# The products of P with V, formed in 16 wide matmuls per batch with four slabs of P as one stationary operand

## The chip, the core and the metric

The kernel runs on one NeuronCore of a Trainium2 chip. The metric is the time of one execution on the device, in microseconds (us); 121.49 us is the median of three runs before the change (121.39 to 121.63). TensorE (PE in the profile) multiplies a stationary operand, which it loads first (PEld), with a moving operand and adds up in PSUM. VectorE is DVE, ScalarE is ACT, GpSimd is POOL, and SyncE (SP) issues nearly all of the loads.

## The reference

One decoding step: 8 sequences (batch b), one query position each, 32 query heads in 8 key/value heads of 4, head size 128, and a window of the last 1024 of 4096 cached positions.

```python
xn = _layernorm(x)                                   # x: [8, 1, 512]
q  = (xn @ wq) as [8, 32 heads, 1, 128]
k, v = the last W = 1024 positions of k_cache, v_cache, each head repeated 4 times
p  = softmax(q @ k.T * 128 ** -0.5)
s  = (p @ v) as [8, 1, 4096] @ wo
g  = silu((gelu(xn @ w_gate) * (xn @ w_up)) @ w_down)
out = x + s * g
```

All inputs are bf16. The caches in the window are 2 MB of K and 2 MB of V for each batch.

## The kernel before

The order of instructions on every engine is the order in which the program is written (a manual schedule), and each engine works in that order. Buffers come from pools that turn round; the framework puts in the semaphore waits.

**Loads.** Every large load goes through SP's queue: K and V of a batch in two pieces of 1 MB each (line 73; g = 0 and 1, four key/value heads each), the weights in pieces of 1 to 2 MB. They land in a ring of eight slots of 2 MB, `slot(name)`. A slot is loaded again when its last reader is done: for a K slot that is the second `turn_k` of its batch on DVE, for a V slot the products of its batch on PE. Besides that, the loads share eight completion semaphores, and a load is issued only when the load that used its semaphore before has landed.

**Layout.** A slot holds a batch so that partition p has C = 32 positions (c) of one key/value head of each of two head groups g; it is head p % 4 of the group. One slab is the 128 values of one c. The scores of a batch lie in one PSUM tile, 1024 columns of 128 partitions, in which partition 32 j + h has query head h at a quarter j of the positions, for all four key/value heads of a group; columns of heads that are not its own are set to minus 1e30 (L285). DVE's transposes of 32 x 32 blocks make `kT` of K and `pT` of the exponentials `P_sb`.

**The loop over batches.** With b the batch whose softmax is formed, the body of the loop issues

```python
        load_k(b + 2); load_v(b + 1); turn_k(b + 1, 0)   # SP; SP; DVE L235
        softmax(b)            # DVE L306, L311, L313; ACT L316 four times, L318
        scores(b + 1, 0)      # PE L285 twice, L296 eight times
        gather(b - 1)         # PE L361, L365
        turn_k(b + 1, 1); scores(b + 1, 1)               # DVE L235; PE L296
        turn_p(b)             # DVE L329
        values(b)             # PE L340
        keep_o(b)             # ACT L353
```

and after batch 4 also `regroup(0)` (DVE L376, L378, PE L389, DVE L392), which divides the outputs of batches 0 to 3 by the sums and turns them for the product with `wo`.

**Products with V.** `values(b)` goes over two groups and 32 slabs. For slab c the stationary operand is a 128 x 32 piece of `pT` (32 query heads; the weight is zero where a partition holds a key/value head that is not the query head's own) and the moving operand is the slab's 128 columns of V. The output goes to the 32 partitions that start at 32 (c % 4), so four matmuls that follow each other use four separate quarters of the array's columns; eight slabs are added up in each quarter. `O_ps` has two buffers of one PSUM bank. `keep_o` copies its 128 x 256 values to `O_sb` (fp32), and `gather` adds the four quarters and picks the group's own heads by multiplying with a selection matrix `sel` in fp32; line 365 does the same for the sums of the softmax.

**After the loop** come `gather(7)`, `regroup(1)`, then the feed-forward part: `z_ps` and `u_ps` (L451), the GELU chain on ACT and DVE (L461 to L474), `f_ps` (L480), the sigmoid part (L488 to L492), the product with `wo` in four parts of 32 matmuls (L499), y and out (L507, L509) and the store (L511). PE does `z_ps` only after `r_ps` of `regroup(1)`.

Of the kernel before, what the change touches and what calls it, by code (L numbers as in the profile page):

```python
# [8 lines left out]
ALU = mybir.AluOpType  # L9
AX = mybir.AxisListType  # L10
BF16 = mybir.dt.bfloat16
FP32 = mybir.dt.float32
I32 = mybir.dt.int32
PSUM = bass.MemoryType.PSUM
# [7 lines left out]
def kernel(  # L22
# [13 lines left out]
    nc = tc.nc  # L36

    B, Sq, D = A_x.shape
    Hkv, Sk, Dh = A_k_cache.shape[1], A_k_cache.shape[2], A_k_cache.shape[3]
    Hq = A_wq.shape[1] // Dh  # L40
# [5 lines left out]
    P = nc.NUM_PARTITIONS  # L46
    NK = D // P
    HG = 4
    NG = Hkv // HG
    C = W * HG // P  # L50
# [6 lines left out]
    consts = ctx.enter_context(tc.tile_pool(name="consts", bufs=1))  # L57
    keep = ctx.enter_context(tc.tile_pool(name="keep", bufs=1))
    two = ctx.enter_context(tc.tile_pool(name="two", bufs=2))
    ring = ctx.enter_context(tc.tile_pool(name="ring", bufs=N_SLOTS))  # L60

    def slot(name):
        return ring.tile([P, 2 * ROW], BF16, name=name, tag="slot")
# [17 lines left out]
    k_sb, v_sb = {}, {}  # L81
# [10 lines left out]
    for i in range(2):  # L92
        t = slot("wq_sb").rearrange("p (k n) -> p k n", k=NK // 2)
# [6 lines left out]
    ident = consts.tile([P, P], BF16, name="ident")  # L100
    nc.vector.memset(ident, 0.0)
    nc.gpsimd.affine_select(
        out=ident,
        in_=ident,
# [13 lines left out]
        out=xpad,  # L118
        in_=xpad,
# [17 lines left out]
        out=xhat,  # L137
# [9 lines left out]
    with tc.tile_pool(name="ps_x", bufs=1, space=PSUM) as ps_x:  # L147
# [7 lines left out]
        for t in range(4):  # L155
# [4 lines left out]
                start=True,  # L160
                stop=True,
# [5 lines left out]
    qd = Hq // NG  # L167
# [6 lines left out]
        out=hv,  # L174
        in_=hv,
# [7 lines left out]
        out=neg_st,  # L183
        in_=neg_st,
# [8 lines left out]
        out=neg_mv,  # L193
        in_=neg_mv,
# [7 lines left out]


    NU = Hq // 8
    sel = consts.tile([P, NG, Hq], FP32, name="sel")
    nc.vector.memset(sel, 0.0)
    for g in range(NG):
        nc.vector.tensor_reduce(
            out=sel[:, g, g * qd : (g + 1) * qd],
            in_=ident.rearrange("p (t g h) -> p g h t", t=4, g=NG)[:, g],  # L210
            axis=AX.X,
            op=ALU.add,
        )
    own = consts.tile([P, 8], FP32, name="own")
    nc.vector.tensor_reduce(
        out=own, in_=ident.rearrange("p (i e) -> p e i", e=8), axis=AX.X, op=ALU.add
    )
    pick = consts.tile([P, 4 * NU], BF16, name="pick")
    with nc.allow_low_precision(reason="sums of zeros and a single one"):
        nc.vector.tensor_reduce(  # L220
            out=pick, in_=ident.rearrange("p (a e) -> p a e", e=8), axis=AX.X, op=ALU.add
# [22 lines left out]
    with tc.tile_pool(name="ps_q", bufs=1, space=PSUM) as ps_q:  # L244
        q_ps = [ps_q.tile([P, 512], FP32, name=f"q_ps{i}") for i in range(8)]
        for k in range(NK):
            for i in range(8):
# [4 lines left out]
                    start=(k == 0),  # L252
                    stop=(k == NK - 1),
# [19 lines left out]
    pT, S, P_sb, O_ps = {}, {}, {}, {}  # L273
    sums = keep.tile([P, B], FP32, name="sums")

    actx = ExitStack()
    ps_s = actx.enter_context(tc.tile_pool(name="ps_s", bufs=2, space=PSUM))
    ps_o = actx.enter_context(tc.tile_pool(name="ps_o", bufs=2, space=PSUM))
    ps_g = actx.enter_context(tc.tile_pool(name="ps_g", bufs=1, space=PSUM))

    def scores(b, g):
# [50 lines left out]
        )  # L332

    def values(b):
        O_ps[b] = ps_o.tile([P, NG, Dh], FP32, name="O_ps")
        for g in range(NG):
            vv = v_sb[b][:, g].rearrange("p (c d) -> p c d", d=Dh)
            for c in range(C):
                t = c % 4
                nc.tensor.matmul(  # L340
                    O_ps[b][32 * t : 32 * t + 32, g, :],
                    pT[b][:, c // 2, :, c % 2],
                    vv[:, c, :],
                    start=(c < 4),
                    stop=(c >= C - 4),
                )

    o_ps = {}
    O_sb = {}

    def keep_o(b):
        O_sb[b] = two.tile([P, NG, Dh], FP32, name="O_sb")
        nc.scalar.copy(out=O_sb[b], in_=O_ps[b])  # L353

    def gather(b):
        q = b % 4
        if q == 0:
            o_ps[b // 4] = ps_g.tile([P, Dh + 1], FP32, name="o_ps")
        o = o_ps[b // 4][32 * q : 32 * q + 32, :]
        for g in range(NG):  # L360
            nc.tensor.matmul(  # L361
                o[:, 0:Dh], sel[:, g, :], O_sb[b][:, g, :], start=(g == 0), stop=(g == NG - 1)
            )
        for g in range(NG):
            nc.tensor.matmul(  # L365
                o[:, Dh : Dh + 1],
                sel[:, g, :],
                sums[:, b : b + 1],
                start=(g == 0),
                stop=(g == NG - 1),  # L370
            )

    def regroup(q):

# [24 lines left out]
    for b in range(B):  # L399
        if b + 2 < B:  # L400
            load_k(b + 2)
        if b + 1 < B:
            load_v(b + 1)
            turn_k(b + 1, 0)
        softmax(b)
        if b + 1 < B:
            scores(b + 1, 0)
        if b >= 1:
            gather(b - 1)
        if b + 1 < B:  # L410
            turn_k(b + 1, 1)
            scores(b + 1, 1)
        turn_p(b)
        values(b)
        keep_o(b)
        if b == 4:
            regroup(0)
# [10 lines left out]
    for u in range(NU):  # L428
        if u % 2 == 0:
            pair = slot("wo_sb").rearrange("p (v j d) -> p v j d", v=2, d=D)  # L430
        t = pair[:, u % 2]
# [6 lines left out]
        wo.append(t)  # L438

    gather(B - 1)  # L440
    regroup(1)
    actx.close()
# [4 lines left out]
    for n, ws in (("z_ps", wgu[0]), ("u_ps", wgu[1])):  # L447
        ps = ps_f.tile([P, FT], FP32, name=n)
        for k in range(NK):
            for t in range(4):  # L450
# [4 lines left out]
                    start=(k == 0),  # L455
                    stop=(k == NK - 1),
# [6 lines left out]
        out=z2, in0=z2, scalar1=0.044715, scalar2=1.0, op0=ALU.mult, op1=ALU.add  # L463
# [11 lines left out]
        out=hT.rearrange("p j b -> p (j b)"), in_=h_bf.rearrange("p (y j) -> p j y", j=NJ)  # L475
    )
    f_ps = ps_f.tile([P, DT], FP32, name="f_ps")
    for j in range(NJ):
        for t in range(4):
# [4 lines left out]
                start=(j == 0),  # L484
                stop=(j == NJ - 1),
# [4 lines left out]
        out=g_sb, in0=g_sb, scalar1=0.5, scalar2=0.5, op0=ALU.mult, op1=ALU.add  # L490
# [5 lines left out]
    for u in range(NU):  # L496
        for j in range(8):
            for t in range(4):
# [4 lines left out]
                    start=(u == 0 and j == 0),  # L503
                    stop=(u == NU - 1 and j == 7),
# [7 lines left out]
        out=out_f.rearrange("b (t d) -> t b d", t=4), in_=out_sb[0 : P : RB, :]  # L512
# [31 lines left out]
```

## Time and profile before

| | before |
|---|---|
| median of three runs | 121.49 us |
| the profiled execution's own time | 121.48 us |
| its span, first to last instruction | 119.4 us |
| mean granted TensorE clock | 0.838 |
| bytes read from HBM | 47.46 MB, 397 GB/s over the span |
| busy: PE, PEld | 73.0 us (61%), 38.7 us (32%) |
| busy: DVE, ACT, POOL | 75.8 us (63%), 31.4 us (26%), 3.2 us (3%) |

The profiled execution's time is its span and 2.1 us around it. Where lines of the profile are shown, an entry is start and duration in us, then engine, line of the kernel, operation, output and inputs. "x8" counts instructions, a bracket gives the idle time of the engine before the entry and what ended it.

### The profile page before, as it was taken

What the parts mean: (1) busy time and instruction counts of PE and PEld (TensorE: products, weight loads), DVE (VectorE), ACT (ScalarE), POOL (GpSimd) and SP (SyncE); (2) the same over time, 40 slices, a digit from 0 to 9 for tenths busy, and PEclk for the clock granted to TensorE, in tenths of its full rate; (3) what the DMA queues carried; (4) which work ended last, traced back from release to release, by engine and by line L of the source; (5) the groups of instructions that cost most, each with busy time, mean ns of one, the idle gap of its engine ahead of it and who ended that gap; (6) DMA issues with size and microseconds to landing.
All of it is one profiled execution on the core that took longest, in us unless ns stands there. A gap on an engine that the chain in (4) does not pass through costs nothing.

```text
span 119.4 us, 2300 instructions
## 1 busy us (share of the span) xinstructions
PE 73.0 (61%) x985; PEld 38.7 (32%) x992; DVE 75.8 (63%) x101; ACT 31.4 (26%) x75; POOL 3.2 (3%) x10
## 2 busy tenths in 40 slices
PE   0001499811994987969687674991994547545370
PEld 0000134300341544535443351450453433143350
DVE  1048978399739999999959959909943241651000
ACT  2233000676007052341712510700616211200000
POOL 2006100000000000000000000000000000000000
PEclk9999999985599999999999998599589855555555
DMA  1999999999999999999999999999999999999930
GB/s 47 411 445 417 434 425 431 417 428 434 428 420 425 431 423 423 428 423 431 417 431 420 431 423 423 428 428 423 420 434 439 437 433 418 427 421 417 412 148 3
DMA packets 6254, 47.61 MB, mean 399 GB/s; under 512 B 732, under 2 KB 868, under 8 KB 1124
## 3 DMA queue, kind: packets, MB, share of 16 engines
q1 hardware_dynamic: 6228, 47.46, 94.3%
q8 instruction: 8, 0.13, 0.4%
q10 hardware_dynamic: 16, 0.01, 0.0%
q14 instruction: 2, 0.02, 0.0%
HBM read 47.46 MB, written 0.01 MB: 397 GB/s over the span
## 4 chain that ended last, share of the span: by engine, by line
DMA 85%; DVE 6%; PE 4%; SPq 2%; issue 1%
DMA k_sb<-in_A_k_cache_dram 48%; DMA wo_sb<-in_A_wo_dram 20%; DMA v_sb<-in_A_v_cache_dram 17%; DVE kT L235 4%; PE S_ps L296 2%; PE s_ps L499 1%; SPq L73 1%; DVE mx L306 1%; SPq L94 1%; PE O_ps L340 1%; PE r_ps L389 1%; DVE y L507 0%; DVE out_sb L509 0%; DVE oT L392 0%; DVE m L311 0%
## 5 line engine op out<-in xcount | busy, mean ns | idle before, releaser
L296 PE MATMUL S_ps<-kT,qbd 128*128 128x512 bf16 x128 | 34.1, 413 | 15.5 <-DVE kT L235 11.9
L235 DVE STREAM_TRANSPOSE kT<-k_sb 128x2048 int32<-128x2048 int32 x16 | 36.5, 2289 | 4.4 <-DMA k_sb<-in_A_k_cache_dram 4.3
L296 PEld LDWEIGHTS <-qbd 128*128 128x128 bf16 x128 | 12.8, 102 | 31.9 <-issue 16.4
L248 PE MATMUL q_ps<-wq_sb,xnR 128*128 128x512 bf16 x32 | 9.8, 481 | 4.3 <-DMA wq_sb<-in_A_wq_dram 4.3
L316 ACT ACTIVATE nb<-m 32x1 f32<-32x1 f32 x32 | 6.4, 201 | 22.5 <-DVE m L313 22.2
L306 DVE TENSOR_REDUCE mx<-S_ps 128x1 f32<-128x1024 f32 x8 | 9.6, 1196 | 4.1 <-PE S_ps L296 4.1
L318 ACT ACTIVATE P_sb<-S_ps,nb 128x1024 bf16<-128x1024 f32 x8 | 11.1, 1390 | 0.3
L340 PE MATMUL O_ps<-v_sb,pT 128*32 128x128 bf16 x512 | 9.1, 226 | 2.6 <-DVE pT L329 2.6
L340 PEld LDWEIGHTS <-pT 128*32 128x32 bf16 x512 | 7.6, 100 | 5.6 <-issue 3.0
L353 ACT COPY O_sb<-O_ps 128x256 f32<-128x256 f32 x8 | 3.0, 372 | 23.3 <-PE O_ps L340 23.3
L329 DVE STREAM_TRANSPOSE pT<-P_sb 128x512 int32<-128x512 int32 x8 | 5.7, 711 | 3.4 <-ACT P_sb L318 3.3
L248 PEld LDWEIGHTS <-xnR 128*128 128x128 bf16 x32 | 3.7, 118 | 10.1 <-issue 8.1
L361 PE MATMUL o_ps<-O_sb,sel 128*32 128x128 f32 x32 | 6.3, 332 | 0.9 <-ACT O_sb L353 0.9
L499 PE MATMUL s_ps<-wo_sb,oT 128*32 128x128 bf16 x128 | 4.4, 307 | 3.7 <-DMA wo_sb<-in_A_wo_dram 3.7
L258 ACT CAST q_both<-q_ps 128x512 bf16<-128x512 f32 x6 | 3.0, 611 | 12.2 <-PE q_ps L248 12.2
L151 PE MATMUL xnT_ps<-ident,xhat 8*128 8x8 bf16 x4 | 0.3, 174 | 8.9 <-DVE xhat L136 8.9
L499 PEld LDWEIGHTS <-oT 128*32 128x32 bf16 x128 | 3.5, 136 | 4.7 <-issue 4.5
L361 PEld LDWEIGHTS o_ps<-O_sb,sel 128*32 128x32 f32 x32 | 3.4, 128 | 5.0 <-issue 1.7
L507 DVE TENSOR_TENSOR y<-s_ps,g_sb 128x128 f32<-128x128 f32 x1 | 0.3, 292 | 7.2 <-PE s_ps L499 7.2
L285 PE MATMUL S_ps<-neg_mv,neg_st 128*128 128x512 bf16 x9 | 3.3, 384 | 1.9 <-DVE q_both L258 1.9
L129 DVE BATCH_NORM_STATS2 stats<-x_sb 8x6 f32<-8x512 bf16 x1 | 0.7, 681 | 5.7 <-DMA x_sb<-in_A_x_dram 5.7
L240 DVE MEMSET qbd<- 128x4096 uint32 x1 | 3.5, 3472 | 0.8 <-issue 0.8
(64 smaller groups left out, 51.2 us busy)
## 6 DMA issues: line engine op xcount, KB each, us to landing
k_sb<-in_A_k_cache_dram SPq DMA_DIRECT2D x16, 1024.0 KB, 19.7
v_sb<-in_A_v_cache_dram SPq DMA_DIRECT2D x16, 1024.0 KB, 20.0
wq_sb<-in_A_wq_dram SPq DMA_DIRECT2D x2, 2048.0 KB, 11.4
wo_sb<-in_A_wo_dram SPq DMA_DIRECT2D x3, 1024.0 KB, 25.1
wgu_sb<-in_B_w_gate_dram SPq DMA_DIRECT2D x1, 1792.0 KB, 21.4
wgu_sb<-in_B_w_up_dram SPq DMA_DIRECT2D x1, 1792.0 KB
wd_sb<-in_B_w_down_dram SPq DMA_DIRECT2D x1, 1792.0 KB
wo_sb<-in_A_wo_dram SPq DMA_DIRECT2D x1, 640.0 KB
```

The costliest lines, as they stand in the source:

```text
L235: nc.vector.transpose(out=t.bitcast(I32), in_=k_sb[b][:, g].bitcast(I32))
L240: nc.vector.memset(qbd, 0.0)
L248: nc.tensor.matmul(q_ps[i], xnR[:, k, :, :].rearrange("p j b -> p (j b)"), wq_sb[k][:, i * 512 : (i + 1) * 512], start=(k == 0), stop=(k = ...
L285: nc.tensor.matmul(S[b][:, half, :], neg_st.rearrange("p j h -> p (j h)"), neg_mv.rearrange("p a n -> p (a n)"), start=True, stop=False,)
L296: nc.tensor.matmul(S[b][:, half, :], qbd[:, m, b, w, g, :], kv[:, half * 16 : (half + 1) * 16, m, :, w], start=False, stop=(g == NG - 1 an ...
L306: nc.vector.tensor_reduce(out=mx, in_=S[b].rearrange("p a c -> p (a c)"), axis=AX.X, op=ALU.max)
L316: nc.scalar.mul(nb[32 * j : 32 * j + 32, :], m1, -inv)
L318: nc.scalar.activation(out=P_sb[b].rearrange("p c i w -> p c w i"), in_=S[b].rearrange("p a (c w i) -> p (a c) w i", w=2, i=32), func=ACT.Exp,
L329: nc.vector.transpose(out=pT[b].rearrange("p c h w -> p (c h w)").bitcast(I32), in_=P_sb[b].rearrange("p c i w -> p (c i w)").bitcast(I32),)
L340: nc.tensor.matmul(O_ps[b][32 * t : 32 * t + 32, g, :], pT[b][:, c // 2, :, c % 2], vv[:, c, :], start=(c < 4), stop=(c >= C - 4),)
L361: nc.tensor.matmul(o[:, 0:Dh], sel[:, g, :], O_sb[b][:, g, :], start=(g == 0), stop=(g == NG - 1))
L499: nc.tensor.matmul(s_ps[32 * t : 32 * t + 32, :], oT[:, j, u, :], wo[u][:, j, t * DT : (t + 1) * DT], start=(u == 0 and j == 0), stop=(u = ...
```

## The change

`values` no longer puts each slab's product into its own quarter. Four slabs of `pT` that follow each other (4 x 32 = 128 columns) are one stationary operand, and the same four slabs of V (4 x 128 = 512 columns) are the moving operand. The output is 128 x 512: four slabs of P against four slabs of V, of which only the four blocks on the diagonal (P of a slab against V of the same slab) are wanted. Eight such matmuls are added up for each group.

`O_ps` becomes two PSUM banks (one for each group) and has one buffer in place of two. `keep_o` takes two copies: the lower 64 partitions with columns 0 to 255 of both groups and the upper 64 with columns 256 to 511, so that each half holds its two diagonal blocks and two unwanted ones. `sel` gains an axis of two, which names the block that is wanted for each row, and is built from wider reductions; a further matrix `sel_s` serves the sums. `gather` then has four matmuls for the outputs, in place of two, and one for the sums, in place of two.

```diff
-    sel = consts.tile([P, NG, Hq], FP32, name="sel")
+    sel = consts.tile([P, NG, 2, Hq], FP32, name="sel")
     nc.vector.memset(sel, 0.0)
     for g in range(NG):
         nc.vector.tensor_reduce(
-            out=sel[:, g, g * qd : (g + 1) * qd],
-            in_=ident.rearrange("p (t g h) -> p g h t", t=4, g=NG)[:, g],
+            out=sel[:, g, :, g * qd : (g + 1) * qd],
+            in_=ident.rearrange("p (a g h w) -> p g w h a", a=2, g=NG, w=2)[:, g],
...
+    sel_s = consts.tile([P, Hq], FP32, name="sel_s")
+    nc.vector.tensor_reduce(
+        out=sel_s, in_=ident.rearrange("p (j h) -> p h j", j=4), axis=AX.X, op=ALU.add
+    )
...
-    ps_o = actx.enter_context(tc.tile_pool(name="ps_o", bufs=2, space=PSUM))
+    ps_o = actx.enter_context(tc.tile_pool(name="ps_o", bufs=1, space=PSUM))
...
     def values(b):
-        O_ps[b] = ps_o.tile([P, NG, Dh], FP32, name="O_ps")
+        O_ps[b] = ps_o.tile([P, NG, 4 * Dh], FP32, name="O_ps")
         for g in range(NG):
-            vv = v_sb[b][:, g].rearrange("p (c d) -> p c d", d=Dh)
-            for c in range(C):
-                t = c % 4
+            vv = v_sb[b][:, g]
+            for c in range(0, C, 4):
                 nc.tensor.matmul(
-                    O_ps[b][32 * t : 32 * t + 32, g, :],
-                    pT[b][:, c // 2, :, c % 2],
-                    vv[:, c, :],
-                    start=(c < 4),
-                    stop=(c >= C - 4),
+                    O_ps[b][:, g, :],
+                    pT[b][:, c // 2 : c // 2 + 2].rearrange("p c h w -> p (c h w)"),
+                    vv[:, c * Dh : (c + 4) * Dh],
+                    start=(c == 0),
+                    stop=(c == C - 4),
                 )
...
     def keep_o(b):
-        O_sb[b] = two.tile([P, NG, Dh], FP32, name="O_sb")
-        nc.scalar.copy(out=O_sb[b], in_=O_ps[b])
+        O_sb[b] = two.tile([P, NG, 2, Dh], FP32, name="O_sb")
+        for a in range(2):
+            rows = slice(64 * a, 64 * a + 64)
+            nc.scalar.copy(
+                out=O_sb[b][rows].rearrange("p g w d -> p g (w d)"),
+                in_=O_ps[b][rows, :, 2 * a * Dh : 2 * (a + 1) * Dh],
+            )
...
         for g in range(NG):
-            nc.tensor.matmul(
-                o[:, 0:Dh], sel[:, g, :], O_sb[b][:, g, :], start=(g == 0), stop=(g == NG - 1)
-            )
-        for g in range(NG):
-            nc.tensor.matmul(
-                o[:, Dh : Dh + 1],
-                sel[:, g, :],
-                sums[:, b : b + 1],
...
+            for w in range(2):
+                nc.tensor.matmul(
+                    o[:, 0:Dh],
+                    sel[:, g, w, :],
+                    O_sb[b][:, g, w, :],
...
+        nc.tensor.matmul(
+            o[:, Dh : Dh + 1], sel_s, sums[:, b : b + 1], start=True, stop=True
+        )
```

More of the change, by code (lines that the diff above doesn't have):

```diff
@@ L360, in gather @@
         for g in range(NG):
-            nc.tensor.matmul(
-                o[:, 0:Dh], sel[:, g, :], O_sb[b][:, g, :], start=(g == 0), stop=(g == NG - 1)
-            )
-        for g in range(NG):
-            nc.tensor.matmul(
-                o[:, Dh : Dh + 1],
-                sel[:, g, :],
-                sums[:, b : b + 1],
-                start=(g == 0),
-                stop=(g == NG - 1),
-            )
+            for w in range(2):
[3 more added lines that the diff above has]
+                    O_sb[b][:, g, w, :],
+                    start=(g == 0 and w == 0),
+                    stop=(g == NG - 1 and w == 1),
+                )
+        nc.tensor.matmul(
+            o[:, Dh : Dh + 1], sel_s, sums[:, b : b + 1], start=True, stop=True
+        )
     def regroup(q):
```

## The prediction

> **What bounds the kernel now.** I read the page's slices and chain first, to see which stage has which limit, then busy time over one batch, then one batch in order of time. On the page:
>
> ```profile
> DVE  1048978399739999999959959909943241651000
> PEclk9999999985599999999999998599589855555555
> DMA  1999999999999999999999999999999999999930
> DMA 85%; DVE 6%; PE 4%; SPq 2%; issue 1%
> ```
>
> The loads never pause from 3 to 115 us and make up 85% of the chain. So 121.5 us is a floor under any change on PE, and the question is how far PE may fall behind the loads before the end moves. One row is a stretch: from the start of a batch's products with V to the next one's (rows 1 to 3), then the last part (columns: length, busy time and count on PE, PEld, DVE, ACT, POOL, granted clock, DMA share, GB/s).
>
> ```profile
> 54.00:60.76 6.76, 5.77 (x91) 3.19 (x91) 5.52 (x6) 2.61 (x7) 0.00 (x0) 1.00 1.01 427
> 68.97:79.22 10.25, 7.83 (x98) 4.15 (x98) 7.26 (x8) 2.62 (x7) 0.00 (x0) 0.83 1.01 424
> 89.07:93.91 4.84, 1.81 (x74) 1.55 (x73) 2.24 (x4) 2.61 (x7) 0.00 (x0) 1.00 1.04 441
> 107.97:119.40 11.43, 4.39 (x128) 3.38 (x127) 1.10 (x4) 0.28 (x1) 0.00 (x0) 0.50 0.59 239
> ```
>
> The loop begins late (first products at 40.48 us), with K already there, and runs at 6.76 us a batch against about 9.9 us in which a batch's 4 MB arrive: it is catching up. From about 61 us it waits for K (kT from 61.08), at 8 to 10 us a batch, to the last products at 93.91. PE has only about 1 us free in a catch-up round. One round in order of time:
>
> ```profile
> 54.00 1.08 PE L340 MATMUL O_ps<-v_sb,pT 128*32 128x128 bf16 x64
> 55.01 0.39 PE L285 MATMUL S_ps<-neg_mv,neg_st 128*128 128x512 bf16 x1
> 55.13 0.37 ACT L353 COPY O_sb<-O_ps 128x256 f32<-128x256 f32 x1 [2.89 <-PE O_ps L340]
> 55.45 1.90 PE L296 MATMUL S_ps<-kT,qbd 128*128 128x512 bf16 x8
> 56.69 0.84 ACT L316 ACTIVATE nb<-m 32x1 f32<-32x1 f32 x4 [1.19 <-DVE m L313]
> 57.28 0.62 PE L361 MATMUL o_ps<-O_sb,sel 128*32 128x128 f32 x4
> 57.56 1.39 ACT L318 ACTIVATE P_sb<-S_ps,nb 128x1024 bf16<-128x1024 f32 x1
> 58.93 1.90 PE L296 MATMUL S_ps<-kT,qbd 128*128 128x512 bf16 x8 [0.93 <-DVE kT L235]
> ```
>
> The 64 small matmuls take 1.0 us in all (54.00 to the next load of weights at 55.00), 16 ns each: four quarters of the array work at once. Eight matmuls with 512 moving columns take 1.83 us to the hand-over (55.45 to 57.28), 0.22 us apart.
>
> **Products with V.** 16 matmuls of 128 x 512 at 0.22 us, the row of the same form, are 3.5 us where 1.0 was: +2.5 us of PE a batch. At the half clock the same row is 0.43 us (16 in 5.35 us at 29.40), so 6.9 us.
>
> [...]
>
> **Gather.** Four instructions of L361 take 0.62 us, 0.115 apart; the new form has four more and two fewer of L365 (0.05 each): +0.36 us, at the half clock (four in 1.06 us, 0.2 apart) +0.6.
>
> **keep_o.** No row is a 64 x 512 fp32 copy. Nearest above: ACT's 128 x 512 cast from PSUM, 0.61 us, six in 3.03, so two make 1.1 us; nearest below: two of the present copy, 0.74. I take 1.1 (+0.75), in the range 0.75 to 1.3. What is queued behind it on ACT is nb and the exponential of the next batch, which now wait for the products on PE. That chain from the start of values(b): 3.5 + 0.17 to the copy, 1.1, nb 0.84, exponential and sum 1.6, transpose of P 0.71, hand-overs 0.2, together 8.1 us to values(b+1).
>
> **The round.** PE: 5.78 + 2.5 + 0.36 = 8.6 us without a gap. DVE needs 6.7 (two transposes of 2.29, 1.19, 0.31, 0.71) and ACT's chain 8.1, so PE takes over as the limit, ACT 0.5 us behind. One O_ps buffer costs nothing: the copy is done 4.8 us into the round, 3.8 us before the next products. K arrives in time.
>
> **Setup.** Two reductions over twice the input, one more, a wider memset: about +0.7 us on DVE before the first kT at 11.68 (rows 0.37 for 128 x 128, 0.25 for 128 x 64). DVE then idles 2.35 us at 22.75, waiting for q. Nothing on the path; +0.7 if that cover were gone.
>
> **Loads.** SP issues a load only when one of its eight semaphores is back; some also wait for values(b). New ends of values(0) to (4): 44.0, 52.6, 61.2, 69.8, 78.4 us, before the issues that need them (46.4, 56.3, 66.0, 76.0, 80.9). Only the third wo load (about 88) waits for values(5), some 3 us more, with up to 16 us of issued loads in front of it. Zero; 3 us if that cover were gone.
>
> **The sum on the profile's times.** Starts of values(0) to (4): 40.5, 49.1, 57.7, 66.3, 74.9 (before: 40.48, 47.24, 54.00, 60.76, 68.97). In the next round regroup(0) sits between: DVE's copy of r_ps waits on PE behind values(4), and kT of batch 6 is queued behind that copy. This row was 10.25 us with part of it at the half clock; with the additions 13.1, or 11.6 if the clock stays up. I take 12.1: values(5) at 87.0, values(6) at 95.6. The last round has no scores and is the ACT chain, 8.1 (4.84 before): values(7) at 103.7 in place of 93.91. Whether those 16 run at full clock is open (3.5 or 6.9):
>
> ```profile
> 70.49:73.90 3.41, 0.99 (x7) 0.49 (x8) 3.22 (x3) 0.00 (x0) 0.00 (x0) 1.00 1.03 430
> 73.90:77.31 3.41, 3.41 (x14) 1.50 (x12) 3.18 (x5) 2.25 (x6) 0.00 (x0) 0.50 0.99 418
> ```
>
> A stretch with PE busy 0.99 of 3.41 us is followed by half clock; the new wait ahead of values(7) holds 1.1 busy us in 4.6, but the stretch may fall otherwise. I take 5.0: end at 108.7 (95.43 before). From there to z_ps was 3.87 us, with copy and gather now 5.1: 113.8 in place of 99.30. z_ps to the end of f_ps is 8.67 us without a wait for loads on the path: 122.4. The four parts with wo, which stood waiting for loads for 3.74 us, now run together: 4 x 1.04 and 0.1, less 0.8 because PE is then busy without a break and may get full clock: 125.9. From there to the end of the span 3.3: 129.2, plus the 2.1 around it: **131.3 us**. The profiled execution, 121.48, is the median's 121.49 within its spread.
>
> **Rivals.** *More than this* (0.12): the copies take 1.3 us and ACT's chain passes PE's (rounds of 8.9), the clock halves at batch 5 and 7. values(5) at 89.6, (7) at 106.8, its end at 113.7, z_ps 119.2: 137 us. For it: the margin of 0.5 us and two half-clock stretches already there. Against it: PE is busier, so that in the loop it idles less.
>
> *The loads cover it, not slower* (0.06): wide matmuls run closer together here than L296 does. The end has 3.74 us of waits for wo to give, of which 1.2 go to copy and gather after values(7). [...] A busier PE with full clock in the last part of L499 (1.25 us) could give 0.6: 120.9. Against it: every run of L296 at full clock has 0.22.
>
> *Not what it says*: 64 small matmuls left in some form. The built order shows 16 pairs a batch of 128 x 512, so I give it none.
>
> **How the numbers follow.** My forecast has 0.82. Its own ends: everything at full clock with copies of 0.75 us gives values(5) at 86.5, values(7) at 102.8 and its end at 106.3, z_ps at 110.9, 0.75 less in the two products behind it (f_ps ends at 118.8), half of 4.2 for wo: 126.3 us. Half clock from batch 5 on gives values(5) at 88.0, values(7) at 104.7, its end at 111.6, z_ps 116.9, f_ps 125.6: 135.3. The range 126.0 to 135.5 takes in both and the near part of the first rival. About 0.2% (0.24 us) is what a measurement here can tell from no change; faster 0.03, same 0.03 (the second rival's halves), slower 0.94.
>
> **What would show it.** Right: rounds of 8.6 us up to values(4) with PE busy throughout; nb waiting for O_sb's copy; DVE idle before kT of batch 6; values(7) starting near 104; no wait for wo before L499, and DMA falling idle at 115 us with the span going on. [...]

## The result and the profile after

The change makes the kernel slower: 129.73 us (median of six runs, 128.58 to 131.14) against 121.49 (six runs, 121.19 to 121.63), a ratio of 1.066 with a 95% interval of 1.061 to 1.071. One of the six runs (131.14) was in a slower state, and the ratio leaves it out; the median of the other five is 129.58 us. The profiled execution took 129.87 us, its span is 127.8. The forecast was 131.3 us, 126.0 to 135.5.

The page, with the same slices and the chain as before:

```profile
DVE  1049975999299939859589445999533020247311
PEclk9999999995999999999999999589999986999559
DMA  2999999999999999999999999999999999991000
PE 66%; DVE 14%; DMA 9%; ACT 4%; issue 2%; SPq 1%; DVEq 0%; ACTq 0%
```

The chain has changed hands: loads were 85% of it, now PE is 66% and loads 9%. The last three slices have no loads and the span goes on. The same stretches as in the prediction, each from one batch's products to the next one's, then from values(7) to z_ps, to the end of f_ps, and to the end of the span (columns as there):

```profile
57.09:65.58 8.49, 8.44 (x45) 4.21 (x45) 6.54 (x7) 3.41 (x8) 0.00 (x0) 1.00 1.02 425
74.06:86.81 12.75, 10.34 (x53) 5.03 (x52) 9.22 (x9) 3.41 (x8) 0.00 (x0) 0.87 1.01 422
95.30:103.24 7.94, 4.65 (x26) 2.46 (x26) 2.24 (x4) 3.39 (x8) 0.00 (x0) 1.00 1.01 426
103.24:113.09 9.85, 7.00 (x34) 3.46 (x35) 1.45 (x2) 1.16 (x2) 0.00 (x0) 0.83 0.99 414
113.09:121.00 7.91, 3.38 (x98) 2.44 (x100) 4.08 (x7) 1.12 (x2) 0.00 (x0) 0.80 0.30 116
121.00:127.80 6.80, 3.42 (x130) 3.15 (x120) 1.10 (x4) 0.28 (x1) 0.00 (x0) 0.73 0.01 4
```

In a catch-up round PE is busy for 8.44 of 8.49 us; DVE has two idle microseconds. One round in order of time, PE and ACT:

```profile
57.09 3.61 PE L343 MATMUL O_ps<-v_sb,pT 128*128 128x512 bf16 x15
...
60.54 0.59 PE L289 MATMUL S_ps<-neg_mv,neg_st 128*128 128x512 bf16 x2
60.74 1.17 ACT L358 COPY O_sb<-O_ps 64x512 f32<-64x512 f32 x2 [4.97 <-PE O_ps L343]
60.97 1.90 PE L300 MATMUL S_ps<-kT,qbd 128*128 128x512 bf16 x8
61.93 0.84 ACT L320 ACTIVATE nb<-m 32x1 f32<-32x1 f32 x4
...
62.80 1.06 PE L370 MATMUL o_ps<-O_sb,sel 128*32 128x128 f32 x8
```

Products to the next matmul are 3.45 us (57.09 to 60.54), 0.216 a matmul. nb starts as soon as the two copies end, although its input was there at 60.19: ACT's queue has the order that the prediction described.

In the round with regroup(0), 74.06 to 86.81, the wait that the prediction named has grown. From the waits before and after (who waited for whom, us in total, times, the longest):

```profile
DVE oT L392 <- PE r_ps L389: 2.1, 2, 1.4
DVE oT L400 <- PE r_ps L397: 4.1, 2, 3.3
```

At the end, the 128 matmuls with wo no longer wait for their load and follow f_ps in one row, at a granted clock of 0.50 from 121.00 to 124.47 us:

```profile
120.79 3.63 PE L507 MATMUL s_ps<-wo_sb,oT 128*32 128x128 bf16 x128
```

### The profile page after: what moved, and what is told of

The parts are those of the page before. It is cut to its first block, busy times and chain, and to the rows that moved or that the text cites. A ratio compares the mean times of both kernels' runs of the same rounds, so it can differ in the third digit from the quotient of the medians.

```text
span 127.8 us, 1577 instructions
## 1 busy us (share of the span) xinstructions
PE 90.8 (71%) x618; PEld 45.4 (36%) x624; DVE 75.8 (59%) x102; ACT 37.7 (30%) x83; POOL 3.2 (2%) x10
## 4 chain that ended last, share of the span: by engine, by line
PE 66%; DVE 14%; DMA 9%; ACT 4%; issue 2%; SPq 1%; DVEq 0%; ACTq 0%
PE S_ps L300 24%; PE O_ps L343 23%; DMA wq_sb<-in_A_wq_dram 9%; PE q_ps L252 7%; PE o_ps L370 5%; DVE kT L239 3%; PE s_ps L507 3%; DVE qbd L274 2%; ACT O_sb L358 2%; PE S_ps L289 2%; PE f_ps L488 1%; DVE q_both L265 1%; ACT P_sb L322 1%; DVE o_x L386 1%; DVE q_both L262 1%
## 5 line engine op out<-in xcount | busy, mean ns | idle before, releaser
L300 PE MATMUL S_ps<-kT,qbd 128*128 128x512 bf16 x128 | 33.3, 406 | 7.6 <-DVE kT L239 4.2
L343 PE MATMUL O_ps<-v_sb,pT 128*128 128x512 bf16 x124 | 30.4, 395 | 2.2 <-DVE pT L333 2.0
L358 ACT COPY O_sb<-O_ps 64x512 f32<-64x512 f32 x16 | 9.3, 579 | 42.3 <-PE O_ps L343 42.2
L343 PEld LDWEIGHTS <-pT 128*128 128x128 bf16 x128 | 12.8, 100 | 18.3 <-issue 2.4
L370 PE MATMUL o_ps<-O_sb,sel 128*32 128x128 f32 x64 | 8.5, 276 | 2.5 <-ACT O_sb L358 2.5
L370 PEld LDWEIGHTS o_ps<-O_sb,sel 128*32 128x32 f32 x64 | 6.3, 109 | 6.2 <-ACT O_sb L358 3.5
L289 PE MATMUL S_ps<-neg_mv,neg_st 128*128 128x512 bf16 x14 | 4.3, 378 | 1.9 <-DVE q_both L262 1.9
L488 PE MATMUL f_ps<-wd_sb,hT 128*32 128x128 bf16 x56 | 1.7, 312 | 4.5 <-DVE hT L482 4.5
L507 PE MATMUL s_ps<-wo_sb,oT 128*32 128x128 bf16 x128 | 3.6, 314 | 0.0
```

The costliest lines, as they stand in the source:

```text
L289: nc.tensor.matmul(S[b][:, half, :], neg_st.rearrange("p j h -> p (j h)"), neg_mv.rearrange("p a n -> p (a n)"), start=True, stop=False,)
L300: nc.tensor.matmul(S[b][:, half, :], qbd[:, m, b, w, g, :], kv[:, half * 16 : (half + 1) * 16, m, :, w], start=False, stop=(g == NG - 1 an ...
L343: nc.tensor.matmul(O_ps[b][:, g, :], pT[b][:, c // 2 : c // 2 + 2].rearrange("p c h w -> p (c h w)"), vv[:, c * Dh : (c + 4) * Dh], start= ...
L358: nc.scalar.copy(out=O_sb[b][rows].rearrange("p g w d -> p g (w d)"), in_=O_ps[b][rows, :, 2 * a * Dh : 2 * (a + 1) * Dh],)
L370: nc.tensor.matmul(o[:, 0:Dh], sel[:, g, w, :], O_sb[b][:, g, w, :], start=(g == 0 and w == 0), stop=(g == NG - 1 and w == 1),)
L507: nc.tensor.matmul(s_ps[32 * t : 32 * t + 32, :], oT[:, j, u, :], wo[u][:, j, t * DT : (t + 1) * DT], start=(u == 0 and j == 0), stop=(u = ...
```

## The experiments

Every kernel was compared with the kernel before on the same chip in the same session (121.51 to 121.63 us).

**e1: the small matmuls with everything else of the change.**

```diff
 # after the change, but
+    O_all = ps_o.tile([P, NG, 4 * Dh], FP32, name="O_ps")   # set to zero once
...
+                    O_all[32 * t : 32 * t + 32, g, t * Dh : (t + 1) * Dh],
+                    pT[b][:, c // 2, :, c % 2],
+                    vv[:, c, :],
```

> The kernel after the change with the 64 small matmuls per batch put back (each writes its own 32 x 128 diagonal block; the rest of the two PSUM banks is set to zero once). The two copies of 64 x 512, the wider selection and the longer gather stay. Theory (PE's 3.5 us of wide matmuls make PE the limit of a round): PE needs 5.78 + 0.36 = 6.1 us a round, below DVE's 6.7, so rounds of 6.8 us as before; copy and gather put 1.2 us behind the last products, inside the 3.7 us for which the end waits for wo: 121.5 us (121.2 to 122.0). Rival (the larger output, that is the copies on ACT with nb queued behind them, or the single buffer of O_ps, carries the loss): the copy's 0.75 us and the gather's 0.36 us in each of 8 rounds, 124 us or more.

122.85 us, ratio 1.0105 (1.009 to 1.012). The rounds were 6.76 us, so the two copies, the longer gather and the single buffer cost the loop nothing as long as PE has time to spare. But 1.3 us over the kernel before is five times what a measurement can tell, and the expectation had none of it: the last part with wo waited for its load until 116.24 us, 1.4 us later than before. e6 finds out why.

**e2: PE's time alone, as more small matmuls.**

```diff
-            for c in range(C):
+            for i in range(-5 * C // 2, C):
+                c = i % C
```

> The kernel before, with each batch's small matmuls issued three and a half times (224 in place of 64, the last full pass gives the result), so that PE has 3.5 us of products per batch and nothing else of the change is there. Theory: rounds of 5.78 + 2.5 = 8.3 us in place of 6.76; values(4) near 73.6, values(5) near 86, values(7) near 101.6 (ACT chain 7.3 us), its end 106.9 at half clock, z_ps 110.8, total 127.6 us (125.5 to 129). Rival (copies, gather and buffer carry the loss, or wide matmuls hold something else up): 121.5 to 122.5 us.

154.22 us, ratio 1.270 (1.265 to 1.275): missed by 27 us, and useless for the question. The products of batch 1:

```profile
51.88 2.30 PE L341 MATMUL O_ps<-v_sb,pT 128*32 128x128 bf16 x151
57.74 1.69 PE L341 MATMUL O_ps<-v_sb,pT 128*32 128x128 bf16 x73 [3.55 <-issue]
```

After some 150 small matmuls without a break PE stands still for 3.55 us, and no semaphore is what it waits for ("issue"). In batches 0 to 5 there is one such stop each, of 2.87 to 3.64 us; in batch 6 there are two short ones, and the 224 of batch 7 run without one. The same time of PE needs few instructions, so e5 took the place of this run.

**e5: PE's time alone, as 12 wide matmuls that nothing uses.**

```diff
         for g in range(NG):
+            for _ in range(12 * g):
+                nc.tensor.matmul(idle_ps, neg_st..., neg_mv..., start=True, stop=True)
```

> The kernel before with 12 matmuls of 128 x 512 on constants put between the two groups of each batch's products; their output is used by nothing. It is the PE time of the change (12 x 0.216 = 2.6 us a batch) in few instructions, without the wide output, its copies, its gather or its place in SBUF. O_ps has one buffer, to make room. Theory (PE's time alone carries most of the loss): rounds of 5.78 + 2.6 = 8.4 us, values(4) near 74.1, values(5) 86.5, values(7) 102.3, z_ps 111.4, total 127.5 to 129 us. Rival (what else the change adds carries it): 121.5 to 123 us.

127.37 us, ratio 1.050 (1.047 to 1.053); rounds of 8.58 us, a round with regroup(0) of 12.65, z_ps at 111.50:

```profile
56.83:65.41 8.58, 8.58 (x103) 4.21 (x102) 6.53 (x7) 2.51 (x7) 0.00 (x0) 1.00 1.01 423
74.00:86.65 12.65, 9.29 (x111) 4.79 (x110) 7.96 (x9) 2.61 (x7) 0.00 (x0) 1.00 1.01 429
```

From the first product to the next step PE needs 3.82 us (48.24 to 52.06) where it needed 1.0, so the filler added 2.8 us a batch and not 2.6. That is what the wide products and the longer gather add together (2.45 and 0.36). So 5.9 of the 8.2 us come from PE's time alone, with the small copies, the short gather and the slots where they were. Against this run the kernel after the change is 1.6 us later at z_ps (113.09): the last round is 0.64 us longer (7.94 against 7.30), and the way from the last products to z_ps 1.2 us (4.54 against 3.38), where the larger copies and the gather stand in line. It is also 1.1 us slower in the 128 matmuls with wo (3.63 us, at a granted clock of 0.50, against 2.58).

**e3 and e7: half of the widening.** Two slabs in one stationary operand, two matmuls at a time in the two halves of the array; in e7 also 128 bytes ahead of the ring of slots. Both have two O_ps buffers again and one copy per batch.

```diff
-            for c in range(0, C, 4):
+            for c in range(0, C, 2):
+                a = (c // 2) % 2
                 nc.tensor.matmul(
-                    O_ps[b][:, g, :],
+                    O_ps[b][64 * a : 64 * a + 64, g, :],
...
+    shift = keep.tile([P, 32], FP32, name="shift")      # e7 alone
+    nc.vector.memset(shift, 0.0)
```

> Between the two: two slabs of P as one stationary operand (64 columns) and 256 columns of V, 32 matmuls per batch, alternating between the two halves of the array's columns. The output is 128 x 256 per batch and group pair of blocks, one copy of 128 x 512; selection and gather as after the change. Theory: two run at a time, 16 x 0.11 = 1.8 us of products, a round of 5.78 + 0.8 + 0.36 = 6.9 us against DVE's 6.8; values(7) near 95.3 us, z_ps near 102.5, and the parts with wo end with the last load: 121.5 us (121.2 to 122.3). [...] If the halves don't run at once: 3.5 us of products and 128 to 129 us.

> e3 (two slabs per matmul, 32 of 64 x 256) with 128 bytes more ahead of the ring, so that the slots begin at a multiple of 512 again. If the place of the slots cost e3 its 1.2 us: last load near 114.8 us and 121.5 us in all (121.2 to 121.8). If the wider output did: 122.7 us as in e3.

e3 took 122.73 us, e7 121.61 (ratio 1.0009, 0.9997 to 1.002: no difference from the kernel before). The 32 matmuls need 1.87 us a batch (46.45 to 48.32 in e3), 0.058 each, where half of a 512-column matmul is 0.108: two ran at a time. The rounds take 7.0 us, and with products of this length the loads do cover them.

**e6 and e12: where the slots begin.** The kernel before, with a tile of zeros ahead of the ring.

```diff
+    shift = keep.tile([P, 96], FP32, name="shift")      # e6; e12: 512 in place of 96
+    nc.vector.memset(shift, 0.0)
```

> The kernel before with a tile of 384 bytes per partition (96 zeros, read by nothing) ahead of the ring, so that the ring's slots begin at byte 55680 of a partition, 384 past a multiple of 512, where they began at 55296, a multiple of 512. In the kernel after the change, in e1, e3 and e4 they begin 384 past such a multiple; in the kernel before and e2 on one. Theory (where the slots lie sets the rate of the loads): loads of 1 MB every 2.48 us in place of 2.44, the last load of wo near 116.2 us in place of 114.8, total 122.8 us. Rival (the loads of e1 and e3 were slower because of the wider output's traffic or order): 121.5 us.

> The kernel before with 2048 bytes more ahead of the ring, so that its slots begin at a multiple of 4096 (57344) where they began at a multiple of 512 that isn't one of 4096 (55296). If only the place within 512 bytes counts for the loads (theory, from e6 and e7): 121.5 us. If a rounder place makes the loads faster still: below 121.2 us, and a version faster than both kernels.

e6: 122.76 us, ratio 1.0106 (1.009 to 1.012), as expected. Issues of loads on SP, in e6:

```profile
21.24 2.96 SPq L73 DMA_DIRECT2D k_sb<-in_A_k_cache_dram  x2
...
84.26 14.53 SPq L439 DMA_DIRECT2D wo_sb<-in_A_wo_dram  x6
```

Between these two rows lie 63.02 us; in the kernel before it was 62.33 (20.95 to 83.28). Each load is issued when an earlier one lands (in the kernel before, SP's L73 waits 25.3 us for landings of K and 19.2 us for those of V), so this is the rate of the loads: 422 GB/s from 20 to 110 us against 426 (the kernel before, then e6):

```profile
20.00:110.00 90.00, 62.87 (x866) 33.48 (x871) 63.64 (x78) 28.17 (x70) 0.00 (x0) 0.84 1.01 426
20.00:110.00 90.00, 61.28 (x857) 32.29 (x858) 64.33 (x79) 28.16 (x70) 0.00 (x0) 0.86 1.01 422
```

The change's larger `sel` and the new `sel_s` (256 and 128 bytes; the larger `O_sb` adds a multiple of 512) had moved every slot to 384 bytes past a multiple of 512, and that alone costs 1.2 us when the loads set the end. e7 takes it away from e3. It accounts for e1 too, which has the same slots and the same 1.3 us; e1 was not run with its slots moved back. e12: 121.54 us, ratio 0.9991 (0.998 to 1.0002): a multiple of 4096 was no better than one of 512.

**e8: the round with regroup(0).** DVE's copy of r_ps goes behind the next transpose of K.

```diff
+        if b == 5:
+            place(0)          # the copy of r_ps, taken out of regroup
         softmax(b)
```

> The kernel after the change, with DVE's copy of r_ps of regroup(0) put behind the next transpose of K (kT of batch 6) in place of ahead of it. Nothing is left out. Theory: the round from values(4) to values(5), 12.75 us after the change, holds a wait of DVE for PE's r_ps behind values(4), then PE's wait for kT of batch 6 and a stretch at half clock; without them it is 8.5 + 0.7 = 9.2 us, so values(5) starts near 83.3 us, values(7) near 99.7, total 126.2 us (125 to 127). Rival (that round is long for K's arrival or the clock alone): 129 to 130 us.

126.32 us, ratio 1.040 (1.036 to 1.045). The round:

```profile
73.25:83.17 9.92, 9.01 (x54) 4.81 (x53) 8.61 (x9) 3.40 (x8) 0.00 (x0) 1.00 1.01 422
```

9.92 us in place of 12.75, at a granted clock of 1.00, and 3.4 us less in all: the wait was DVE's place in its queue, not K's arrival. It was not the clock alone either, since e5's round took 12.65 us at a granted clock of 1.00.

**e4 and e9: ACT's queue ahead of the last products.** The copy of a batch goes behind the next exponential; the last gather but one goes behind the last products. e4 does it in every round, e9 in the last alone.

```diff
         softmax(b)
+        if b >= 1:            # e9: if b == B - 1
+            keep_o(b - 1)
...
         values(b)
-        keep_o(b)
```

> The kernel after the change, with ACT's copies of a batch's output put behind the next batch's exponential (before, they stood ahead of its nb), and the gather of batch 6 put behind the last products. Nothing is left out. Theory: rounds 0 to 6 stay at 8.5 and 12.8 us, since PE sets them; only the last one shrinks: values(7) starts near 100.1 in place of 103.24 and, with PE idle for only about 1.2 us ahead of it, runs at full clock (3.5 us in place of 5.3); z_ps near 108 in place of 113.1, total 124.7 us (123.5 to 126). Rival (ACT's queue doesn't set the last round, PE's own amount does): 129 to 130 us.

> The kernel after the change, with the new order of e4 in the last round alone: ACT copies batch 6's products behind batch 7's exponential, and PE gathers them behind batch 7's products. In e4 the same order made PE wait 3 us for the copy in the round with regroup(0). Theory: nothing moves up to values(6) at 95.3 us; values(7) then starts 5.2 us later (in e4 5.24; after the change 7.94) and runs at full clock, 3.5 us in place of 5.3: 129.7 less 2.7 and 1.8, so 125.2 us (124.5 to 126.2). Rival (the last round is set by something else): 129 us or more.

e4 took 128.76 us, a miss. The last round did as expected (5.24 us, and 3.61 us for the products, as in the loop at a granted clock of 1.00), but in the round with regroup(0) a new wait stood on PE: the gather of batch 4 waited 2.98 us for the copy, which was now queued behind an exponential that was itself late. e9, without that, took 125.48 us, ratio 1.032 (1.030 to 1.035):

```profile
100.73 3.61 PE L343 MATMUL O_ps<-v_sb,pT 128*128 128x512 bf16 x16 [1.62 <-ACT O_sb L358]
```

The last products start 5.23 us after those of batch 6 (7.94 after the change) and take 3.61 us in place of 5.31.

**e10: e8 and e9 together, the slots on a multiple of 512.** The wide matmuls stay.

> e8 and e9 together, with 128 bytes more ahead of the ring, so that the slots begin at a multiple of 512 as before. The wide matmuls stay, 3.5 us a batch, and nothing is left out. Theory: values(5) near 83.2 us, values(6) 91.7, values(7) 97.0, z_ps 105.1, f_ps ends at 112.7; the parts with wo end with the last load (114.8 us) or up to 0.5 us later: 121.5 us (120.9 to 122.2). Rival (the wide matmuls cost time wherever they stand): 123 us or more.

122.81 us, ratio 1.010 (1.008 to 1.012): 0.6 us outside the expected range. z_ps starts at 104.83 and f_ps ends at 112.7, as expected, but the end came late:

```profile
112.53 3.08 PE L523 MATMUL s_ps<-wo_sb,oT 128*32 128x128 bf16 x105
116.28 0.63 PE L523 MATMUL s_ps<-wo_sb,oT 128*32 128x128 bf16 x23 [0.67 <-issue]
```

The parts with wo follow f_ps without a break, at 0.029 us a matmul (0.028 after the change, at a granted clock of 0.50), and then PE stops for 0.67 us on "issue", after 161 small matmuls in a row (56 of f_ps, 105 here). e2 stopped after a like number, 145 to 167. The profiled execution took 122.31 us, 0.8 more than that of the kernel before, and the stop is most of it; the 0.5 us by which the median is later still can't be read from this profile.

**e11: a busy PE in the last part of the kernel before.**

```diff
+    keep_busy(12)             # 128 x 512 matmuls ahead of f_ps
...
+        if u < NU - 1:
+            keep_busy(4)      # behind each part with wo but the last
```

> The kernel before with matmuls of 128 x 512 that nothing uses in PE's waits of the last part: 12 ahead of f_ps and 4 behind each of the first three parts with wo. The prediction's second rival named a busier PE at full clock in the last 32 matmuls with wo (1.25 us before) as a gain of 0.6 us. Theory (the clock is granted after a stretch of full work and kept at half work): the last part takes 0.6 to 0.7 us, total 120.9 us (120.7 to 121.2). Rival (the clock stays at half, or the filler delays the parts): 121.5 us or more.

121.59 us, ratio 1.0002 (0.999 to 1.001). The clock went up as the theory expected. The weight loads of the fillers, which begin at 103.39 us, come 0.43 us apart up to 105.50, and from 105.85 five of them within 0.96 us. After that f_ps took 0.96 us in place of 1.69 and the first three parts 0.63 in place of 1.04, with PE busy for 1.67 of the 2.43 us from one part to the next. The mean granted clock was 0.929 in place of 0.838. The end did not move, and the chain of e11 shows why. Below it stands the last part with wo, first in the kernel before, then in e11:

```profile
93.08 22.34 DMA wo_sb<-in_A_wo_dram
115.42 0.04 issue
115.46 0.30 PE s_ps L512 x8
115.79 0.26 PE s_ps L512 x4
```

```profile
114.84 1.25 PE L499 MATMUL s_ps<-wo_sb,oT 128*32 128x128 bf16 x32 [0.49 <-DMA wo_sb<-in_A_wo_dram]
114.86 1.18 PE L512 MATMUL s_ps<-wo_sb,oT 128*32 128x128 bf16 x32
```

The load of the last part comes in three pieces (640, 256 and 128 KB). In e11 its last twelve matmuls start only at 115.46 us, 0.04 behind the landing of a piece, and the last four of these at 115.79. In the kernel before the part took 1.25 us at a granted clock of 0.50, where each of the three others took 1.04; in e11 it took 1.18, though PE was fast enough for 0.63. So the pieces' arrival set the end in e11, and there was nothing to win.

No version beat the kernel before; e7, e11 and e12 equal it.

## Why the prediction was right

**Who sets the end.** PE took the chain over from the loads, by 8.2 us where 9.8 was forecast. e1 and e5 show it from both sides: without the wide matmuls the rest of the change adds nothing but the slots' 1.2 us; with PE's time alone 5.9 us appear. The remaining 2.3 us (2.7 between the two profiled spans) have no run of their own; by the traces they are the larger copies and the gather, which stand on the path behind batches 6 and 7 once PE sets the pace, and the slower products with wo (3.63 us against 2.58). The signs that the prediction gave came: rounds near 8.6 us with PE busy throughout, nb behind the copies, DVE idle ahead of kT of batch 6, values(7) near 104 us, no wait for wo, the span going on after the loads. The granted clock was 0.80 and 0.73 in the last two stretches (113.09 to 127.80), where the kernel before had 0.50 from 107.97 us on.

**The terms.** Products 3.45 us (3.5 taken), 0.216 each. Copies 1.17 (1.1), gather 1.03 from the first L370 to the next scores (1.0 by the sum). Rounds 8.49 (8.6). The round with regroup(0) was 12.75 us (12.1 taken, 11.6 to 13.1 as its ends), and e8 confirms its mechanism. Its low end was too low: in e5 the clock stayed up (1.00) and the round still took 12.65 us, because PE then waited 1.16 us for DVE's second transpose of K. The last round was 7.94 us (8.1), through the queue on ACT that e9 takes away. Products of batch 7: 5.31 us, between 3.5 and 6.9 (5.0 taken, a guess between the two, so that it fits is luck). The row that the prediction gives for half clock, 16 matmuls in 5.35 us, is a mixed one, for the granted clock was 0.50 up to 32 us and 1.00 from 33 us on; the 0.43 us is the spacing of the first.

**Errors that cancelled.** values(4) started 0.84 us earlier than forecast (74.06 against 74.9), and the round behind it took 0.65 us more, so that values(5) fits to 0.2. The four parts with wo were to take 4 x 1.04 and 0.1, less 0.8 for a full clock: 3.46 us. They took 3.47, but at a granted clock of 0.50: in one row 32 matmuls take 0.87 us, and 1.04 was what a part takes by itself. The size was right and its reason was not.

**The term that was off.** From z_ps to the end of f_ps I had 8.67 us from the kernel before; it took 7.91, because z_ps ran at a granted clock of 1.00 (0.94 us in place of 1.69 at 0.50). With the 0.7 us by which z_ps itself came earlier than forecast, that is 1.5 of the 1.6 us by which the forecast was high. The low end of the prediction's range had this gain in it, the forecast itself did not.

**The rival in which the loads cover it** needed wide matmuls closer together than L296's 0.22 us, and no run shows that: after the change they came 0.216 us apart, which is about the same. With the products at 1.87 us a batch, two matmuls at a time (e7), the time is that of the kernel before. Its gain of 0.6 us from a full clock in the last part was a misread row: I took the 1.25 us of the last L499 for work alone, and its last piece of the load comes so late that the faster clock of e11 won nothing (121.59 us).

**What was missed.** "Loads: zero" left out that new tiles move the ring. After the change it doesn't show in the profile, where PE sets the end; the kernel's floor had nevertheless gone from 121.5 to about 122.8 (e6), and a version that is bound by loads pays it.

## What to carry to other kernels

A matmul that computes more than is wanted was paid for here in columns that pass through PE: 16 of 512 cost 3.5 us where 64 of 128 in four quarters at once cost 1.0, although there are a quarter as many instructions; 32 of 256 in two halves cost 1.87 (e3). All pass the same 8192 columns of V; what the change gave up is that four matmuls ran at a time. Whether that counts is decided by the slack of the round in which the kernel catches up with its loads (1 us here), not by the share of busy time, and with an engine at its limit, waits that were free before (a copy ahead of the next softmax, a small copy ahead of a transpose) turn up on the path and can be ordered away: e8 and e9 took back 3.4 and 4.3 us one by one. Look, too, at where a changed tile moves the buffers behind it.

## What was not expected of the hardware

- Loads into slots that begin 384 bytes past a multiple of 512 in a partition ran at 422 GB/s against 426, 1.2 us on this kernel; a multiple of 512 or of 4096 made no difference (121.58 and 121.54 us). Other offsets weren't tried.
- PE stopped on "issue" in rows of small matmuls without a break: in e2 after 145 to 167 of them, for 2.87 to 3.64 us at a time, and again for 0.38 and 1.48 us at 121 to 125 us; in e10 after 161, for 0.67 us. What PE waited for is not shown. The number of matmuls doesn't decide by itself: e9, with 184 in a row at the end (56 of f_ps, 128 with wo), shows no such stop.
